# Moving the spare product bank and the first scores of the next unit inside the Mish stretches of a fused attention kernel

## The chip, the cores and the metric

The kernel runs on one core of one Trainium2 chip. A core has five engines, each with its own instruction stream, which wait for each other through semaphores: TensorE (PE in the profile; its weight loads are PEld) multiplies, VectorE (DVE), ScalarE (ACT) and GpSimd (POOL) compute elementwise, SyncE (SP) issues transfers. TensorE writes to PSUM, eight banks of 128 x 512 floats, which VectorE and ScalarE read. The metric is the device time of one execution in microseconds; before the change the median of three runs is 489.91 us (489.81 to 490.08).

## What is computed

Attention over 8 batches of 12 heads, 448 positions and 64 features, with one more term in the softmax's denominator, and on its output a feed-forward layer with the Mish function between its two products:

```python
scores = scale * np.matmul(q, k.transpose(0, 1, 3, 2))
m = np.max(scores, axis=-1, keepdims=True)
e = np.exp(scores - m)
attn = e / (np.sum(e, axis=-1, keepdims=True) + np.exp(-m) + 1e-09)
x = np.matmul(attn, v)                # then 3584 tokens x 768
...
h = x @ w_in                          # 768 x 2048
sp = np.where(h > 20.0, h, np.log1p(np.exp(np.minimum(h, 20.0))))
out = (h * np.tanh(sp)) @ w_out       # 2048 x 768
```

Inputs and output are float32; the matrix products run in bfloat16.

## The kernel before

**Tiling.** Heads are taken in pairs, 48 in all, and three pairs make a unit (sixteen units, two for each batch). The 896 query rows of a pair are seven tiles of 128; their scores are made in four steps, of two, two, two and one tile. A step writes one of three score tiles `sc_tiles` (two PSUM banks each), in turn, so a unit's twelve steps use each tile four times, and the next unit begins with `sc_tiles[0]` again. The last two PSUM banks are `mo_tiles`, handed out by `mo_take` (L107) from a queue, the longest free first; both products of the feed-forward layer and the transposes of the first pairs use them.

**The attention stage of a unit** (L551 to L585). For each of twelve steps ScalarE takes the exponentials of a finished score step (`exps`, L275), then TensorE works off the step's share of the second product (`mm2_part`, L417) for earlier batches, and then `scores_ahead` (L222) issues the scores of coming steps as score tiles come free, each followed by a row maximum on VectorE (L270). At the fourth step of each pair TensorE multiplies an earlier pair's transposed weights by its values into the second bank of that step's score tile (`av_pair`, L344). VectorE's copies out of PSUM are not issued with the product but kept in the list `late`, and issued at the next `flush_late`.

**The Mish stretch between two attention stages** (L591 to L611) goes through eight blocks, `f` = 0 to 7. Each block is one call of `mm1_mish` (L375): a flush of `late`, six matmuls of the first product into one bank (L382), and one Mish activation on ScalarE from there (L388). The bank is taken from `mo_tiles` and given back at once to the queue's end, except in one block, the spare one, which uses the first bank of `sc_tiles[0]`. The first of the two `mo_tiles` in turn is free when the stretch begins; the other still holds the last part of the second product, whose copy (L433) is issued by block 0's flush.

Around the blocks the stretch also does, in program order, which is the order on every engine's queue:

- behind block 0: the denominators of the unit just finished (L296, L300, VectorE) and the normalisation of its first pair (L317, seven VectorE instructions), then the DMA that transposes that pair (L321, issued by SP);
- behind blocks 1, 3 and 5: the eight transposes of a pair of the next unit (`transpose_pair`, L179) into banks of `sc_tiles[2]` and `sc_tiles[1]`, and their copies (`evac_qk`): `qd` by VectorE (L210, two instructions, with the scale), `kT` by ScalarE (L218);
- behind block 3, ahead of that block's transposes: the first score step of the next unit, into `sc_tiles[0]`, with its row maximum;
- further behind block 3: the normalisation of the second pair on VectorE and its transposing DMA;
- behind block 4: the normalisation of the third pair on POOL (L315), ahead of which VectorE copies a small tile for it (L308), and its DMA;
- behind blocks 6 and 7: the second and third score step of the next unit, into `sc_tiles[1]` and `sc_tiles[2]`.

The program has sixteen Mish stretches. The first thirteen do all of this; in the fourteenth there is no next unit any more, and the last two have product blocks alone.

Of the kernel before, what the change touches and what calls it, by code (L numbers as in the profile page):

```python
# [19 lines left out]
def kernel(  # L20
# [24 lines left out]
    FF_U = FF_T // UNITS_PER_B  # L45
    NH = d_model // 2
    SCALE = 1.0 / float(D) ** 0.5
    N_PAIRS = B * HP
    STEPS = 4
# [53 lines left out]
    def flush_late():  # L103
        while late:
            late.popleft()()

    def mo_take():  # L107

        if not mo_free:
            flush_late()  # L110
        return mo_free.popleft()
# [33 lines left out]
    def load_w(n):  # L145
        for _ in range(min(n, len(pieces))):
            dst, src = pieces.popleft()
            nc.gpsimd.dma_start(out=dst, in_=src.rearrange("(a p) c -> p a c", p=128))
# [38 lines left out]
    def evac_qk(p, act=False):  # L187
        if p >= N_PAIRS:
            return
        (q_ps, k_ps), own = qkT[p]  # L190
        mo_free.extend(own)
        qd = q_diag[p % 3]
        kT = qk_pool.tile([128, S], BF16, tag="kT", name="kT")
        if p < DIAG_FROM:
            qT = qd.rearrange("d i h r -> d (i h r)")[:, 0:S]
            qkT[p] = (qT, kT)
            if act:
                nc.scalar.mul(qT, q_ps[:, 0:S], SCALE)
            else:
                nc.vector.tensor_scalar(  # L200
                    out=qT, in0=q_ps[:, 0:S], scalar1=SCALE, scalar2=None, op0=ALU.mult
                )
        else:
            qkT[p] = (qd, kT)
            if p < DIAG_FROM + 3:
                nc.vector.memset(qd[0:64, :, 1, :], 0.0)
                nc.vector.memset(qd[64:128, :, 0, :], 0.0)
            for h in range(2):
                rows = slice(64 * h, 64 * h + 64)
                nc.vector.tensor_scalar(  # L210
                    out=qd[rows, :, h, :],
                    in0=q_ps[rows, 0:S].rearrange("d (i r) -> d i r", i=QB),
                    scalar1=SCALE, scalar2=None, op0=ALU.mult,
                )
        if p == 0 or own and not act:
            nc.vector.tensor_copy(out=kT, in_=k_ps[:, 0:S])
        else:
            nc.scalar.copy(kT, k_ps[:, 0:S])  # L218
# [3 lines left out]
    def scores_ahead(limit):  # L222

        while rg["next"] < limit and rg["used"] < len(sc_tiles):
            rg["used"] += 1
            scores(rg["next"])
            rg["next"] += 1
# [147 lines left out]
    def mm1_mish(b, ff):  # L375
        if ff == 0:
            gT[b] = gT_pool.tile([128, FF_T, S], BF16, tag="gT", name="gT")
        flush_late()
        spare = ff % FF_U == 2
        h_ps = sc_tiles[0][:, 0, :] if spare else mo_take()  # L380
        for dm in range(DM_T):
            nc.tensor.matmul(  # L382
                h_ps[:, 0:S],
                lhsT=w_in_sb[:, dm, ff * 128 : (ff + 1) * 128],
                rhs=xT[b][:, dm, :],
                start=(dm == 0), stop=(dm == DM_T - 1),
            )
        nc.scalar.activation(out=gT[b][:, ff, :], in_=h_ps[:, 0:S], func=AF.Mish)  # L388
        if not spare:
            mo_free.append(h_ps)  # L390
# [26 lines left out]
    def mm2_part(g, i, q0, nq):  # L417

        b0, b1 = 2 * g, 2 * g + 1
        cols, n_cols = slice(q0 * NQ, (q0 + nq) * NQ), nq * NQ  # L420
        st = {}
        if i < 3:
            src, c0 = gT[b0], i * 128
        elif i == 3:
            src, c0 = mids[g], 0
        else:
            src, c0 = gT[b1], i * 128 - S

        def evac():
            if (g, i) not in o_sbs:  # L430
                o_sbs[g, i] = [o_pool.tile([128, d_model], FP32, tag="o_sb", name="o_sb"), 0]
            o_sb, have = o_sbs[g, i]
            nc.vector.tensor_copy(out=o_sb[:, cols], in_=st["o"][:, 0:n_cols])  # L433
            mo_free.append(st["o"])
            o_sbs[g, i][1] = have + nq
            if (g, i) == (B // 2 - 1, 6):
                store_rows(g, i, o_sb, cols)
            elif have + nq == 4:
                store_rows(g, i, o_sb, slice(0, d_model))

        def chunk(f0, f1):
            if f0 == 0:
                flush_late()
                st["o"] = mo_take()
            for ff in range(f0, f1):
                nc.tensor.matmul(  # L446
                    st["o"][:, 0:n_cols],
                    lhsT=src[:, ff, c0 : c0 + 128],
                    rhs=w_out_sb[:, ff, cols],
                    start=(ff == 0), stop=(ff == FF_T - 1),  # L450
                )
            if f1 == FF_T:
                late.append(evac)

        step = 2
        return [(lambda f0=f0: chunk(f0, f0 + step), nq) for f0 in range(0, FF_T, step)]
# [83 lines left out]
    for u in range(UNITS_PER_B, N_UNITS + 2 * UNITS_PER_B):  # L540
        attn = u < N_UNITS
        filler = deque()
        for part in plan.get(u, []):
            filler.extend(mm2_part(*part))
        total, done, acc = sum(w for _, w in filler), 0, 0.0
        p0 = u * UNIT_PAIRS
        if attn and u >= first_mm2:
            av_with.update({p0 + i: p0 + i - UNIT_PAIRS for i in range(UNIT_PAIRS)})
        end = min((u + 1) * UNIT_PAIRS, N_PAIRS) * STEPS

        for n in range(steps):  # L551
            pi, s = divmod(n, STEPS)
            p, idx = p0 + pi, p0 * STEPS + n
            late_tp = u == UNITS_PER_B and n == STEPS
            if late_tp:
                transpose_pair(p0 + 2)
            exps(idx)
            if late_tp:
                evac_qk(p0 + 2)
            if u == UNITS_PER_B + 1:  # L560
                for part in TURN_AT[1].get(n, []):
                    turn_on_pe(*part)
            flush_late()
            acc += weight[n]
            want = int(total * acc / sum(weight) + 1e-6)
            while done < want:
                fn, w = filler.popleft()
                fn()
                done += w
            scores_ahead(end)  # L570
            if n in LOAD_AT:
                load_pair(p0 + LOAD_AT.index(n) + LEAD)
                cast_pair(p0 + LOAD_AT.index(n) + LEAD - 1)
            if u - UNITS_PER_B < len(AV_AT):
                early = AV_AT[u - UNITS_PER_B]
                if n in early:
                    av_pair(early[n])
                if u == UNITS_PER_B:
                    for part in TURN_AT[0].get(n, []):
                        turn_on_pe(*part)  # L580
            elif s == (2 if pi else 0) and N_PAIRS <= p < N_PAIRS + UNIT_PAIRS:
                av_pair(p - UNIT_PAIRS)
            if u - UNITS_PER_B < len(W_AT):
                load_w(W_AT[u - UNITS_PER_B].get(n, 0))
        assert done == total  # L585

        moe = u < N_UNITS + UNITS_PER_B
        b, w = (u - UNITS_PER_B) // UNITS_PER_B, u % UNITS_PER_B
        nxt = p0 + UNIT_PAIRS
        todo = sorted(range(p0, nxt), key=lambda p: p in BY_PE)  # L590
        for f in range(FF_U):  # L591
            if moe:
                mm1_mish(b, w * FF_U + f)
            if u == UNITS_PER_B and f in (2, 6):
                load_w(1)
            if not attn:
                continue
            if f == 0:
                denominators(att[p0]["whole"])
                normalise(todo[0], dma=todo[0] not in BY_PE)  # L600
            if f == 3:
                scores_ahead(min(nxt * STEPS + 1, N_PAIRS * STEPS))
            if f in (1, 3, 5):
                transpose_pair(nxt + f // 2, bank=f // 2 % 2)
                evac_qk(nxt + f // 2)
            if f >= FF_U - 2:
                scores_ahead(min(nxt * STEPS + f - FF_U + 4, N_PAIRS * STEPS))
            if f == 3:
                normalise(todo[1], dma=todo[1] not in BY_PE)
            if f == 4:  # L610
                normalise(todo[2], dma=todo[2] not in BY_PE, on_pool=True)  # L611
        if moe and w == UNITS_PER_B - 1:
            gather_mid(b)
# [32 lines left out]
```

## Time and profile before

| | before |
|---|---|
| median of three runs | 489.91 us |
| the profiled execution, in all | 492.75 us |
| its span, first to last instruction | 491.0 us |
| mean granted TensorE clock | 0.997 |
| TensorE busy | 450.5 us, 92% |
| VectorE busy | 351.3 us, 72% |
| ScalarE busy | 350.2 us, 71% |
| GpSimd busy | 161.5 us, 33% |

All times in the profile are microseconds from the span's start unless they are marked ns. A row of a timeline gives start and length, the engine, the line of the kernel, the operation, what is written and read, the shape, how many instructions were merged (x6), and in brackets the idle time ahead of it with what ended it. A matmul is drawn until its modelled end, which lies behind the start of the next; for the time that TensorE needs, the starts are compared.

### The profile page before, as it was taken

To read this page: it belongs to the slowest core of one execution; us is meant where nothing else is said; L and a number is where in the kernel's file an instruction comes from. 1 tells how busy PE (TensorE), PEld (TensorE's weight loads), DVE (VectorE), ACT (ScalarE), POOL (GpSimd) and SP (SyncE) were. 2 spreads that over 40 slices of the span, in tenths; PEclk is the share of its full clock that TensorE was granted. 3 is DMA by queue.
4 is the path that set the end of the run, shared out by engine and by line. 5 is a ranking of instruction groups with operands and counts; after the bars stand their busy time and mean duration, and the time that the engine had idled before them with its cause. 6 is when DMAs were issued, how large, how long until landed. Compare 5 with 4: busy or idle time off the path is not lost.

```text
span 491.0 us, 8804 instructions
## 1 busy us (share of the span) xinstructions
PE 450.5 (92%) x2992; PEld 248.5 (51%) x2992; DVE 351.3 (72%) x702; ACT 350.2 (71%) x906; POOL 161.5 (33%) x266
## 2 busy tenths in 40 slices
PE   3556898798989999999999999999999999999996
PEld 1222444454644555555655555555556565556563
DVE  4798987978868787878788786878797878420021
ACT  4889678878777887979796878888797979502300
POOL 3622257454412534253413323253425230300000
PEclk9999998999999999999999999999999999999999
DMA  8999999999999999999998979998999686780112
GB/s 212 183 205 228 236 207 221 228 177 236 175 225 263 195 220 188 241 186 267 148 248 187 223 164 210 211 213 227 176 265 179 167 176 140 132 159 21 45 37 93
DMA packets 209452, 92.19 MB, mean 188 GB/s; under 512 B 166272, under 2 KB 205952, under 8 KB 209408
## 3 DMA queue, kind: packets, MB, share of 16 engines
q1 hardware_dynamic: 201920, 85.35, 81.2%
q0 software_dynamic: 7488, 6.29, 8.8%
q8 instruction: 23, 0.38, 0.3%
q14 instruction: 21, 0.17, 0.1%
HBM read 45.61 MB, written 11.01 MB: 115 GB/s over the span
## 4 chain that ended last, share of the span: by engine, by line
PE 68%; DVE 14%; ACT 9%; DMA 4%; issue 2%; SPq 1%; POOL 0%; DVEq 0%; ACTq 0%
PE mo L446 24%; PE mo L382 23%; PE sc L249 8%; ACT en L283 8%; DVE negm L270 7%; PE sc L358 6%; DVE en L317 4%; PE sc L382 3%; PE sc L179 3%; DMA eT<-en 3%; DMA k_f<-in_k_dram 1%; PE mo L358 1%; PE sc L255 1%; DVE xT L367 1%; DVE eT L336 1%
## 5 line engine op out<-in xcount | busy, mean ns | idle before, releaser
L283 ACT ACTIVATE en<-sc,negm 128x448 bf16<-128x448 f32 x336 | 209.7, 637 | 28.7 <-DVE negm L270 16.3
L270 DVE TENSOR_REDUCE negm<-sc 128x2 f32<-128x896 f32 x192 | 182.4, 969 | 61.5 <-PE sc L249 48.7
L446 PE MATMUL mo<-w_out_sb,gT 128*128 128x384 bf16 (+1 forms) x896 | 142.1, 303 | 0.0
L382 PE MATMUL mo<-xT,w_in_sb 128*128 128x448 bf16 x672 | 140.2, 352 | 0.9 <-DVE xT L367 0.9
L388 ACT ACTIVATE gT<-mo 128x448 bf16<-128x448 f32 x112 | 59.4, 543 | 73.5 <-PE mo L382 73.3
L446 PEld LDWEIGHTS <-gT 128*128 128x128 bf16 x896 | 84.0, 98 | 46.8 <-issue 1.3
L382 PEld LDWEIGHTS <-w_in_sb 128*128 128x128 bf16 x768 | 72.8, 98 | 64.9 <-issue 4.2
L315 POOL TENSOR_SCALAR en<-en,rden 128x448 bf16<-128x448 bf16 x98 | 61.7, 649 | 115.8 <-DVE rden L308 106.0
L249 PE MATMUL sc<-kT,qd 128*128 128x448 bf16 x252 | 71.6, 354 | 1.8 <-DVE qd L210 1.5
L162 POOL CAST q_bf<-q_f 112x512 bf16<-112x512 f32 x47 | 29.1, 619 | 121.8 <-DMA q_f<-in_q_dram 105.4
L283 ACT ACTIVATION_READ_ACCUMULATOR en<-sc,negm 128x1 f32 x336 | 69.2, 206 | 0.0
L317 DVE TENSOR_SCALAR en<-en,rden 128x448 bf16<-128x448 bf16 x238 | 67.2, 354 | 0.9
L433 DVE COPY o_sb<-mo 128x384 f32<-128x384 f32 (+1 forms) x64 | 32.1, 502 | 41.3 <-PE mo L446 41.2
L249 PEld LDWEIGHTS <-qd 128*128 128x128 bf16 x252 | 24.0, 97 | 32.1 <-issue 13.9
L358 PE MATMUL sc<-eT,v_bf 112*64 112x448 bf16 x288 | 34.1, 357 | 4.1 <-ACT en L283 2.0
L164 POOL CAST v_bf<-v_f 112x512 bf16<-112x512 f32 x48 | 29.6, 618 | 20.6 <-DMA v_f<-in_v_dram 19.1
L358 PEld LDWEIGHTS <-v_bf 112*64 112x64 bf16 x384 | 21.1, 114 | 25.7 <-issue 16.9
L255 PE MATMUL sc<-kT,qd 64*128 64x448 bf16 x36 | 17.5, 508 | 17.4 <-ACT en L283 16.0
L163 POOL CAST k_bf<-k_f 112x512 bf16<-112x512 f32 x47 | 29.2, 622 | 6.7 <-DMA k_f<-in_k_dram 5.9
L210 DVE TENSOR_SCALAR qd<-sc 64x448 bf16<-64x448 bf16 x72 | 27.8, 386 | 0.9
L218 ACT COPY kT<-sc 128x448 bf16<-128x448 bf16 x39 | 20.8, 534 | 6.8 <-PE sc L179 6.8
L446 PE MATMUL mo<-w_out_sb,mid 128*128 128x384 bf16 x128 | 24.9, 326 | 0.0
(50 smaller groups left out, 306.9 us busy)
## 6 DMA issues: line engine op xcount, KB each, us to landing
q_f<-in_q_dram SPq DMA_DIRECT2D x48, 224.0 KB, 5.5
k_f<-in_k_dram SPq DMA_DIRECT2D x48, 224.0 KB, 5.6
v_f<-in_v_dram SPq DMA_DIRECT2D x48, 224.0 KB, 5.9
w_in_sb<-in_moe_w_in_dram POOLq DMA_DIRECT2D x12, 256.0 KB, 5.6
w_out_sb<-in_moe_w_out_dram POOLq DMA_DIRECT2D x8, 384.0 KB, 8.6
out_dram<-o_sb SPq DMA_DIRECT2D x7, 336.0 KB, 3.5
out_dram<-o_sb SPq DMA_DIRECT2D x8, 288.0 KB, 4.8
out_dram<-o_sb SPq DMA_DIRECT2D x8, 240.0 KB, 3.4
```

The source lines that it names most:

```text
L163: cast_k(out=k_bf, in_=k_f.rearrange(by_t, t=NT))
L164: nc.gpsimd.tensor_copy(out=v_bf, in_=v_f)
L249: nc.tensor.matmul(sc[:, bk, 0:S], lhsT=qT[:, i].rearrange("d h r -> d (h r)"), rhs=kT, start=True, stop=True,)
L270: nc.vector.tensor_reduce(out=negm, in_=sc[:, 0 : len(cols), 0:S], axis=AX.X, op=ALU.max, negate=True)
L283: nc.scalar.activation(out=st["en"][:, :, c, 0:SP_], in_=sc[:, bk, 0:S].rearrange("q (j c) -> q j c", j=NT), func=AF.Exp, bias=st["negm"][ ...
L315: nc.gpsimd.tensor_scalar(scalar2=1.0, op0=ALU.mult, op1=ALU.mult, **args)
L317: nc.vector.tensor_scalar(scalar2=None, op0=ALU.mult, **args)
L358: nc.tensor.matmul(av[h * 64 : (h + 1) * 64, 0:S], lhsT=v_bf[:, h, j * D : (j + 1) * D], rhs=e_h, start=(j == 0), stop=(j == NT - 1),)
L382: nc.tensor.matmul(h_ps[:, 0:S], lhsT=w_in_sb[:, dm, ff * 128 : (ff + 1) * 128], rhs=xT[b][:, dm, :], start=(dm == 0), stop=(dm == DM_T - 1),)
L388: nc.scalar.activation(out=gT[b][:, ff, :], in_=h_ps[:, 0:S], func=AF.Mish)
L433: nc.vector.tensor_copy(out=o_sb[:, cols], in_=st["o"][:, 0:n_cols])
L446: nc.tensor.matmul(st["o"][:, 0:n_cols], lhsT=src[:, ff, c0 : c0 + 128], rhs=w_out_sb[:, ff, cols], start=(ff == 0), stop=(ff == FF_T - 1),)
```

## The change

The spare block, whose product goes to the first bank of `sc_tiles[0]`, is block 1 and not block 2, so block 2 takes the second of the `mo_tiles` where block 1 took it. From block 3 on the banks are as before. The next unit's first score step is issued behind block 4 and not behind block 3; on TensorE it moves past the transposes of the next unit's second pair and block 4's matmuls. On VectorE its row maximum moves past that pair's two scalings and the second pair's normalisation. Nothing else moves.

```diff
@@ -376,7 +376,7 @@
         if ff == 0:
             gT[b] = gT_pool.tile([128, FF_T, S], BF16, tag="gT", name="gT")
         flush_late()
-        spare = ff % FF_U == 2
+        spare = ff % FF_U == 1
         h_ps = sc_tiles[0][:, 0, :] if spare else mo_take()
         for dm in range(DM_T):
             nc.tensor.matmul(
@@ -598,11 +598,11 @@
             if f == 0:
                 denominators(att[p0]["whole"])
                 normalise(todo[0], dma=todo[0] not in BY_PE)
-            if f == 3:
-                scores_ahead(min(nxt * STEPS + 1, N_PAIRS * STEPS))
             if f in (1, 3, 5):
                 transpose_pair(nxt + f // 2, bank=f // 2 % 2)
                 evac_qk(nxt + f // 2)
+            if f == 4:
+                scores_ahead(min(nxt * STEPS + 1, N_PAIRS * STEPS))
             if f >= FF_U - 2:
                 scores_ahead(min(nxt * STEPS + f - FF_U + 4, N_PAIRS * STEPS))
             if f == 3:
```

## The prediction, made before the changed kernel was run

> **What bounds the kernel now.** I read the page first: the span, and the chain of work that ended last.
>
> ```profile
> span 491.0 us, 8804 instructions
> PE 68%; DVE 14%; ACT 9%; DMA 4%; issue 2%; SPq 1%; POOL 0%; DVEq 0%; ACTq 0%
> ```
>
> Two thirds of the end are set by TensorE, so the question is where TensorE still stands still inside the Mish stretches. The program has sixteen of them. I took their bounds from the TensorE timeline (first product matmul of the stretch to first matmul after it) and asked for TensorE's busy time in each; the rows give from:to, length, busy time, the matmuls touched, granted clock, DMA share, GB/s. These are the first fourteen.
>
> ```profile
> 65.89:77.99 12.10, 11.54 (x81) 1.00 1.02 180
> 93.84:105.63 11.79, 11.70 (x78) 1.00 1.18 182
> 120.54:132.31 11.77, 11.58 (x81) 1.00 1.31 193
> 149.20:161.94 12.74, 11.74 (x80) 1.00 1.08 259
> 176.88:188.44 11.56, 11.56 (x79) 1.00 0.84 169
> 203.39:215.14 11.75, 11.74 (x80) 1.00 0.85 199
> 230.25:241.66 11.41, 11.41 (x81) 1.00 0.79 180
> 256.61:268.62 12.01, 11.73 (x79) 1.00 0.87 190
> 283.92:295.48 11.56, 11.56 (x80) 1.00 0.72 151
> 310.43:321.99 11.56, 11.56 (x80) 1.00 0.95 199
> 337.09:348.62 11.53, 11.53 (x80) 1.00 0.84 185
> 363.57:375.13 11.56, 11.56 (x80) 1.00 0.90 182
> 390.07:401.64 11.57, 11.57 (x81) 1.00 0.66 134
> 416.59:425.87 9.28, 9.28 (x50) 1.00 0.48 90
> ```
>
> Thirteen stretches do the same work, eight product blocks, three transposed pairs and three scores, at a granted clock of 1.00, yet they last from 11.41 to 12.74 us. The busy column hides this, because a matmul is drawn longer than its turn; lengths and starts are what to read. The shortest, at 230.25, shows TensorE's timeline with no stall.
>
> ```profile
> 230.25 2.43 PE L382 MATMUL mo<-xT,w_in_sb 128*128 128x448 bf16 x12
> ...
> 232.91 1.30 PE L382 MATMUL sc<-xT,w_in_sb 128*128 128x448 bf16 x6
> ...
> 235.19 0.54 PE L249 MATMUL sc<-kT,qd 128*128 128x448 bf16 x2
> 235.56 0.36 PE L179 MATMUL sc<-ident,q_bf 112*128 112x112 bf16 x4
> ```
>
> From start to start: blocks 2 and 3 take 2.28 us (232.91 to 235.19), so one takes 1.14; blocks 0 and 1 with the first transposed pair take 2.66 (230.25 to 232.91), so the pair takes 0.38; a score step takes 0.37 (235.19 to 235.56). Eight blocks, three pairs and three scores make 9.12 + 1.14 + 1.11 = 11.4: that stretch is saturated. Now the one at 256.61, 0.60 longer: TensorE and its weight loads, then VectorE, then ScalarE.
>
> ```profile
> 256.61 2.59 PE L382 MATMUL mo<-xT,w_in_sb 128*128 128x448 bf16 x12
> 257.90 0.85 PEld L382 LDWEIGHTS <-w_in_sb 128*128 128x128 bf16 x5 [0.25 <-issue]
> 259.43 1.30 PE L382 MATMUL sc<-xT,w_in_sb 128*128 128x448 bf16 x6
> 260.56 1.30 PE L382 MATMUL mo<-xT,w_in_sb 128*128 128x448 bf16 x6
> 262.14 0.55 PE L249 MATMUL sc<-kT,qd 128*128 128x448 bf16 x2 [0.28 <-DVE qd L210]
> ...
> 268.24 0.54 PE L249 MATMUL sc<-kT,qd 128*128 128x448 bf16 x2
> ```
>
> ```profile
> 257.30 0.55 DVE L433 COPY o_sb<-mo 128x384 f32<-128x384 f32 x1
> 259.25 2.12 DVE L317 TENSOR_SCALAR en<-en,rden 128x448 bf16<-128x448 bf16 x7
> 261.30 0.78 DVE L210 TENSOR_SCALAR qd<-sc 64x448 bf16<-64x448 bf16 x2
> 262.73 1.09 DVE L270 TENSOR_REDUCE negm<-sc 128x2 f32<-128x896 f32 x1 [0.65 <-PE sc L249]
> ...
> 264.55 1.81 DVE L317 TENSOR_SCALAR en<-en,rden 128x448 bf16<-128x448 bf16 x7
> ```
>
> ```profile
> 256.09 0.20 ACT L283 ACTIVATION_READ_ACCUMULATOR en<-sc,negm 128x1 f32 x1
> 257.48 0.63 ACT L283 ACTIVATE en<-sc,negm 128x448 bf16<-128x448 f32 x1
> 259.62 0.98 ACT L388 ACTIVATE gT<-mo 128x448 bf16<-128x448 f32 x2
> 260.90 0.57 ACT L388 ACTIVATE gT<-sc 128x448 bf16<-128x448 f32 x1
> ```
>
> There are two stalls. **Stall A**, at block 1: its product tile is the one that the last output part still occupies, and VectorE's copy out of it ends at 257.85. The second half of its weights resumes at 257.90. Block 2 starts 2.82 behind block 0 (256.61 to 259.43), and 2.66 in the stretch without a stall, so the wait is 0.16. **Stall B**, at the first score, behind block 3: that block is through at 260.56 + 1.14 = 261.70, but the score needs qd, whose two scalings stand on VectorE behind seven normalisations and end at 262.08. The score starts at 262.14: 0.44 lost. A and B make the 0.60.
>
> **The change part by part.** No instruction is added or removed; none of what moves issues a DMA.
>
> *Block 1 takes the score tile's bank.* It needs the exponentials of the unit's tenth step, whose accumulator read ends at 256.29. Block 1 is due at 256.61 + 1.14 = 257.75, so the margin is 1.46 us and A is gone. Block 2 takes the late product tile at 259.28 (with the transposes ahead of it), 1.4 us after that copy. I count A in the stretches at 149.20, 176.88, 203.39, 256.61, 283.92, 310.43, 363.57, 390.07 and 416.59; in those at 230.25 and 337.09 the last part is a narrow one whose copy ends earlier, and A is absent.
>
> *Block 3 then comes 0.16 earlier, at 260.41,* and needs the Mish of block 0. That pair of Mish instructions starts at 259.62 and the second ends at 260.60; one of them alone takes about 0.54, so the first ends near 260.17. Margin 0.24, of which a semaphore takes 0.05 (262.08 to 262.14 above). I take zero; the other bound is that all of A comes back here, 0.16 in each of nine stretches. Block 4's tile now waits for block 2's Mish, which stands behind block 1's and a copy of kT and ends by 261.47; block 4 is due at 261.94. Nothing is lost.
>
> *The first score moves behind block 4,* to 261.94 + 1.14 = 263.08, a full 1.0 us after qd at 262.08. The cover is one transposed pair and one block, 1.52 us. The longest B is that at 149.20, where the seven normalisations are slow beside POOL's casts:
>
> ```profile
> 151.78 2.92 DVE L317 TENSOR_SCALAR en<-en,rden 128x448 bf16<-128x448 bf16 x7
> 152.27 0.62 POOL L162 CAST q_bf<-q_f 112x512 bf16<-112x512 f32 x1 [0.88 <-DMA q_f<-in_q_dram]
> ```
>
> There the normalisations end at 154.70 and the two scalings (0.78) near 155.48; the score will be due 6.47 behind the stretch's start (256.61 to 263.08), at 155.67. It fits.
>
> *Behind the moved score on VectorE.* The score's row maximum now stands behind the second pair's scaling and normalisation instead of ahead of them; then come the small copy for POOL and the third qd. At 256.61: second scaling to 262.9, normalisation (1.81) to 264.7, maximum (1.09) to 265.8, 0.2 allowed for the copy to 266.0, third qd (0.78) to 266.8. The last score needs that qd and is due at 267.64: margin 0.85. The middle pair's transposing DMA can start up to 1.6 us earlier (its normalisation ends at 264.7, not 266.36); POOL's normalisation moves with the stretch. No order on SP's or POOL's queue changes. The first exponentials of the next unit stand behind the last Mish and a table load, 2 us after all of this.
>
> A rule that speaks against this: by the Trainium skill, page "SBUF — State Buffer", section "Who interferes with whom", a VectorE tensor_scalar in a two-port mode and a GpSimd instruction lock each other out for a whole instruction. The 2.92 row above, against 1.81 without casts beside it, agrees in kind. With three casts of 0.62 each in full on the moved normalisation, an estimate from that rule, the third qd would be 1.86 late and the last score 1.0.
>
> **The sum.** Stretches 149.20 to 390.07 are ten; their lengths sum to 117.25, ten times 11.41 is 114.10, so 3.15 goes, and 0.16 at 416.59: **3.3 us**. Does it stay gone? The attention stage between two stretches lasts 176.88 - 161.94 = 14.94, 203.39 - 188.44 = 14.95, 256.61 - 241.66 = 14.95, 310.43 - 295.48 = 14.95: the same behind a stretch of 12.74 as behind one of 11.41. It hangs on the stretch's end alone, so what a stretch saves is saved. For the first three stretches (0.69, 0.38 and 0.36 over 11.41) it is less clear, since one transfer is late behind them:
>
> ```profile
>   DMA eT<-en: 1.9, 1
> ...
> DMA to landing us min/median/max: 6.0/6.4/12.4
> ```
>
> This is the only wait of TensorE for a transposed pair, and the stage behind 132.31 is the one that it stretches (149.20 - 132.31 = 16.89, 1.94 over 14.95); I take the longest landing, 12.4 us where 6.4 is the median, for this transfer's. The 0.36 of the stretch at 120.54 comes after that transfer's issue and is swallowed. The other two, 0.69 + 0.38 = 1.07 at most, move that issue earlier. If the landing follows, 1.1 is kept; if the DMA engines (share 1.31 there) land it at the same time, none. I take 0.6, nearer to the first, since the loads that crowd it move with the program. Together 3.9 us of 491.0. The profiled execution took 492.75 in all, the median of the three runs is 489.91; the stalls are the same program's, so I take the 3.9 off the median: **486.0 us**.
>
> **The rivals.**
>
> *Block 3 takes A back and the early part is lost.* If Mish of block 0 ends after 260.36 there, block 3 waits. For it: the margin of 0.24 is the smallest here. Against: with A gone, the stretch at 230.25 already runs block 3 at this distance and shows no wait. Only B of the ten stretches is left, 3.15 - 8 x 0.16 = 1.9: 488.0 us.
>
> *The saving reappears elsewhere.* The DMA queues are busy throughout (shares of 0.66 to 1.31 above), so transfers might hold the units at their present pace. Against: one DMA wait of TensorE in the whole run. Then 489.9.
>
> *Slower: the tile that is called free isn't.* If block 1's bank were released only by the unit's last exponential (257.48 + 0.63 = 258.11, read out about 0.1 later), block 1 would start near 258.25, not 257.75: 0.5 in each of the eleven stretches from 149.20 on, 5.5 us, against 3.9 gained: 491.5. It decides from 0.36 a stretch (3.9 / 11). Against: the bank's own last reader ends at 256.29, the twelfth step being in another tile.
>
> *Casts meet the moved normalisation.* At the measured 2.92 instead of 1.81 the third qd is 1.11 late, 0.26 beyond its margin; in some six stretches that have casts at their head, 1.5 given back: 487.5. Against: three casts from 152.27 on end near 154.1, and the second normalisation there begins some 2 us later. By the rule of the Trainium skill's page "SBUF — State Buffer", with 1.0 in each of six, it would be 492.0, an estimate.
>
> **How the numbers follow.** The forecast gets 0.77, the loss at block 3 0.08, the reappearance 0.06, the busy bank 0.05, the casts 0.04. Low end: all stalls of the first three stretches kept, 3.3 + 1.43 = 4.7, 485.2, and 0.2 for spread: 485.0. High end: the first rival's 488.0 and 0.2: 488.2. What is left out is the two last outcomes at 489.9 and beyond, 0.11. A change of 0.2%, 1 us, is about what a measurement of this kernel can tell from none. Faster by more than that: 0.77 + 0.08 + 0.04 = 0.89, less a little for a case I don't see, 0.88; within it 0.06; slower 0.06.
>
> **What would show it.** Right: every stretch up to 390.07 about 11.4 us long; the twelve matmuls before the first transposes split in a mo and a sc group, no pause of weights at block 1; no wait of the first score for qd; attention stages still 14.95. Wrong: a pause ahead of block 1 or block 3, the last score waiting for qd, attention stages longer than 14.95, or the transposed pair behind the third stretch landing at the same time as before.

## The result and the profile after

The changed kernel takes 487.79 us (median of 17 runs, 485.11 to 490.55) against 489.91 us for the kernel before, measured beside it (17 runs, 488.45 to 492.12). The ratio is 0.9953, 95% interval 0.9936 to 0.9970: 1.5 to 3.1 us less. The time lies in the forecast's range and on its side; the 3.9 us of the forecast were too many. The spread of single runs is wide, in part because the start varies: in fourteen profiles of this study the first Mish stretch begins between 62.7 and 65.9 us, though up to there the order of work is the same in all of them. Of the 6.4 us between the spans 491.0 and 484.6, 2.6 are such a difference at the start (65.89 against 63.28) and have nothing to do with the change.

The page after:

```profile
span 484.6 us, 8804 instructions
PE 72%; DVE 12%; ACT 7%; DMA 5%; issue 2%; SPq 1%; POOL 0%; DVEq 0%; POOLq 0%
```

TensorE's share of the chain is 72% here and was 68% before, but nothing follows from that: second profiles of the two kernels have 66% and 69%, the other way round. The lengths of the stretches decide. The same view of the first fourteen Mish stretches as before (from:to, length, TensorE's busy time, clock, DMA share, GB/s):

```profile
63.28:75.06 11.78, 11.63 (x81) 1.00 1.04 177
90.93:102.41 11.48, 11.48 (x79) 1.00 1.37 198
117.54:128.94 11.40, 11.40 (x80) 1.00 1.31 188
144.93:157.29 12.36, 11.56 (x79) 1.00 1.09 273
172.23:183.64 11.41, 11.41 (x81) 1.00 0.94 171
198.59:209.99 11.40, 11.40 (x79) 1.00 0.83 187
225.10:236.50 11.40, 11.40 (x80) 1.00 0.91 190
251.45:262.97 11.52, 11.52 (x80) 1.00 0.90 196
278.26:289.67 11.41, 11.41 (x81) 1.00 0.80 166
304.62:316.02 11.40, 11.40 (x79) 1.00 0.94 190
331.13:342.54 11.41, 11.41 (x82) 1.00 0.90 199
357.49:368.89 11.40, 11.40 (x79) 1.00 1.00 184
383.83:395.24 11.41, 11.41 (x80) 1.00 0.75 146
410.19:419.47 9.28, 9.24 (x50) 1.00 0.48 90
```

Most stretches are at the forecast's 11.4 us. Three rows are not as forecast: the fourth is still 12.36, the eighth 11.52, and the fourteenth has not moved from 9.28. The fourth, on TensorE and then on VectorE:

```profile
147.59 2.44 PE L382 MATMUL mo<-xT,w_in_sb 128*128 128x448 bf16 x12
150.83 0.36 PE L179 MATMUL sc<-ident,q_bf 112*128 112x112 bf16 x4 [0.80 <-DVE qd L210]
151.22 1.30 PE L382 MATMUL mo<-xT,w_in_sb 128*128 128x448 bf16 x6
152.35 0.54 PE L249 MATMUL sc<-kT,qd 128*128 128x448 bf16 x2
```

```profile
147.21 2.87 DVE L317 TENSOR_SCALAR en<-en,rden 128x448 bf16<-128x448 bf16 x7
149.99 0.78 DVE L210 TENSOR_SCALAR qd<-sc 64x448 bf16<-64x448 bf16 x2
```

Blocks 2 and 3 run through without a wait, and the first score, moved behind block 4, doesn't wait either. What waits are the transposes of the next unit's second pair, which now stand directly behind block 3, where the score stood: they start at 150.83, just after the first pair's scalings end at 150.77. They don't read what those scalings write, and they write the other bank of the tile that the scalings read. In the order of TensorE's instructions the wait for VectorE has moved from the score to them. The list gives the first instructions of each group (`Ldweights` a weight load, `Matmult` a matmul) with the engine whose semaphore they wait for, first of the kernel before, then of the changed one; the transposes' weight loads, which wait for POOL's casts in both, are left out:

```
L249 Ldweights qd0                     waits for VectorE
L249 Matmult   sc0 <- kT, qd0          waits for ScalarE
L179 Matmult   sc2 <- ident, q_bf      no wait

L179 Matmult   sc2 <- ident, q_bf      waits for VectorE
...
L249 Matmult   sc0 <- kT, qd0          no wait
```

In the fourteenth stretch the rows show why block 3 is late. TensorE's three rows begin block 0, block 1 and block 2; ScalarE's row is the Mish of block 0.

```profile
410.19 1.30 PE L382 MATMUL mo<-xT,w_in_sb 128*128 128x448 bf16 x6
411.33 1.30 PE L382 MATMUL sc<-xT,w_in_sb 128*128 128x448 bf16 x6
412.46 2.82 PE L382 MATMUL mo<-xT,w_in_sb 128*128 128x448 bf16 x13
```

```profile
413.21 0.54 ACT L388 ACTIVATE gT<-mo 128x448 bf16<-128x448 f32 x1
```

Block 1 has no pause any more, but there are no transposes behind it in this stretch, so block 3 is due at 412.46 + 1.14 = 413.60, ahead of the end of block 0's Mish at 413.75. It takes back what block 1 saved.

The transposed pair that was late behind the third stretch is still late, by less: TensorE waits 1.0 us for it (1.9 before), and the longest landing is 11.6 us (12.4 before).

```profile
  DMA eT<-en: 1.0, 1
...
DMA to landing us min/median/max: 6.1/6.5/11.6
```

### The profile page after: what moved, and what is told of

Its sections match the earlier page's. It is cut to its first block, busy times and chain, and to the rows that moved or that the text cites. A ratio compares the mean times of both kernels' runs of the same rounds, so it can differ in the third digit from the quotient of the medians.

```text
span 484.6 us, 8804 instructions
## 1 busy us (share of the span) xinstructions
PE 448.3 (93%) x2992; PEld 249.0 (51%) x2992; DVE 347.1 (72%) x702; ACT 348.8 (72%) x906; POOL 160.6 (33%) x266
## 4 chain that ended last, share of the span: by engine, by line
PE 72%; DVE 12%; ACT 7%; DMA 5%; issue 2%; SPq 1%; POOL 0%; DVEq 0%; POOLq 0%
PE mo L446 25%; PE mo L382 24%; PE sc L249 8%; DVE negm L270 7%; ACT en L283 6%; PE sc L358 6%; PE sc L382 3%; PE sc L179 3%; DMA eT<-en 2%; DVE en L317 2%; DMA k_f<-in_k_dram 1%; PE mo L358 1%; DMA q_f<-in_q_dram 1%; PE sc L255 1%; DVE eT L336 1%
## 5 line engine op out<-in xcount | busy, mean ns | idle before, releaser
L283 ACT ACTIVATE en<-sc,negm 128x448 bf16<-128x448 f32 x336 | 209.3, 636 | 26.9 <-DVE negm L270 15.2
L388 ACT ACTIVATE gT<-mo 128x448 bf16<-128x448 f32 x112 | 61.2, 547 | 77.4 <-PE mo L382 77.1
L249 PE MATMUL sc<-kT,qd 128*128 128x448 bf16 x252 | 71.5, 354 | 0.3 <-ACT en L283 0.2
L317 DVE TENSOR_SCALAR en<-en,rden 128x448 bf16<-128x448 bf16 x238 | 64.2, 343 | 0.9
L249 PEld LDWEIGHTS <-qd 128*128 128x128 bf16 x252 | 24.5, 97 | 28.9 <-issue 13.5
L358 PEld LDWEIGHTS <-v_bf 112*64 112x64 bf16 x384 | 20.9, 114 | 24.9 <-issue 16.9
L179 PEld LDWEIGHTS <-q_bf 112*128 112x128 bf16 x192 | 14.5, 104 | 17.8 <-DVE q_bf L162 4.4
```

Source lines behind the costliest of these rows:

```text
L179: nc.tensor.transpose(by_s[s][:, t * SP_ : (t + 1) * SP_], src[:, t].rearrange("p h d -> p (h d)"), ident[:SP_, :SP_],)
L249: nc.tensor.matmul(sc[:, bk, 0:S], lhsT=qT[:, i].rearrange("d h r -> d (h r)"), rhs=kT, start=True, stop=True,)
L283: nc.scalar.activation(out=st["en"][:, :, c, 0:SP_], in_=sc[:, bk, 0:S].rearrange("q (j c) -> q j c", j=NT), func=AF.Exp, bias=st["negm"][ ...
L317: nc.vector.tensor_scalar(scalar2=None, op0=ALU.mult, **args)
L358: nc.tensor.matmul(av[h * 64 : (h + 1) * 64, 0:S], lhsT=v_bf[:, h, j * D : (j + 1) * D], rhs=e_h, start=(j == 0), stop=(j == NT - 1),)
```

## The experiments

Two theories. **Theory 1** is the prediction: stalls A and B are both removed. **Theory 2** is read from the rows above: A is removed, B is passed on to the transposes. Four kernels went together first. Ratios are against the kernel before, run beside them.

**The kernel before, again** (no edit).

> The kernel before once more, for a second profile of it and for the spread. Both theories: 489.9 us within 1.5, stall A of 0.16 us in the nine stretches that had it, stall B in about the same stretches but of other sizes, since it hangs on POOL's casts. The time up to the first Mish stretch (65.89 us in the profile before, 63.28 after) differs from run to run by 2 to 3 us, with no change to the kernel.

Measured: 489.53 us, ratio 0.9993 (0.9967 to 1.0020). The start is at 63.25 us instead of 65.89. Of the ten steady stretches, the fourth to the thirteenth, B occurs in the fourth, seventh, eighth and tenth (0.82, 0.22, 0.14 and 0.21 us), not in the same as before (1.17 in the fourth, 0.17 in the sixth, 0.44 in the eighth, 0.11 in the eleventh). B is a stall of changing place and size, and one profile's list of it can't be carried over stretch by stretch. POOL's casts beside the normalisations are only one of its causes: in the eighth and tenth stretch here the seven normalisations take the usual 1.81 us, but begin 2.67 and 2.74 us after the stretch's start instead of 2.28, and in the sixth and eleventh of the profile before it is the same (1.81 us, begun at 2.70 and 2.48).

**The change, again** (no edit).

> The changed kernel once more. Theory 1 (the prediction): A and B are both gone, 486.0 us, and the pause of 0.97 us in the stretch at 144.93 was a chance of one run. Theory 2: the second pair's transposes, which now stand in TensorE's order where the score stood, wait for the same qd scalings; A is gone, B is not. Then every stretch with slow normalisations shows a pause ahead of those transposes, block 3 waits about 0.2 us in the fourteenth stretch, and the time is 487.5 to 488.5 us.

Measured: 487.22 us, ratio 0.9968 (0.9945 to 0.9990). The pause ahead of the second pair's transposes is there again, in the fourth, fifth, seventh and eighth stretch: 0.26, 0.30, 0.17 and 0.52 us, 1.3 in sum. It was no chance of one run. The fourteenth stretch lasts 9.29. This is the pattern of theory 2; the time is 0.3 us below the range that it gave.

**Only the spare block.**

```diff
-        spare = ff % FF_U == 2
+        spare = ff % FF_U == 1
```

> The spare block is block 1, the first score stays behind block 3. Theory 1: only A goes, 1.4 us less at most, B stays, so 488.5 us, and the change is 1.9 us or more faster than this. Theory 2: this is all that the change does, so it is as fast as the change within 0.5 us; where B exists A's 0.16 is swallowed by it.

**Only the first score.**

```diff
-            if f == 3:
-                scores_ahead(min(nxt * STEPS + 1, N_PAIRS * STEPS))
             if f in (1, 3, 5):
                 transpose_pair(nxt + f // 2, bank=f // 2 % 2)
                 evac_qk(nxt + f // 2)
+            if f == 4:
+                scores_ahead(min(nxt * STEPS + 1, N_PAIRS * STEPS))
```

> The spare block stays block 2, the first score moves behind block 4. Theory 1: B goes, A stays, 487.4 to 488.0 us, the steady stretches 11.57 us long at most. Theory 2: nothing goes, 489.9 us within 0.5; stretches with slow normalisations still last longer than 11.57 us, with the pause ahead of the second pair's transposes.

Both were run a second time:

> The moved spare block alone, once more: block 1 without a pause, pauses behind block 3 of 2.5 to 3.3 us in all thirteen stretches, third stretch and stage together 28 to 29.4 us, 489 us within 0.7.

> The moved score alone, once more, since one profile is little for a wait whose size changes from run to run. If moving the score takes B away, no pause behind block 3; by theory 2 pauses of 1 to 1.8 us in all thirteen stretches; third stretch and stage together 26.4 to 27.4 us; 488.2 us within 0.7.

Measured: the spare block alone 489.05 and 489.94 us, ratios 0.9998 (0.9973 to 1.0023) and 1.0006 (0.9989 to 1.0022); the score alone 488.20 and 488.55 us, 0.9982 (0.9960 to 1.0004) and 0.9980 (0.9961 to 1.0000). So theory 2's claim that the spare block is all of the change is wrong too: by time the spare block can't be told from nothing. The score's move lowers both medians by some 0.9 us, but its two intervals still reach 1, so it alone isn't clear of noise either; its 488.2 us lies between what the two theories gave. The list of TensorE's waits shows who waits for the scalings of qd, in sum, times and longest, in the first run of the spare block alone:

```profile
PE sc L249 <- DVE qd L210: 2.4, 2, 1.3
```

and in the second run of the score alone:

```profile
PE sc L179 <- DVE qd L210: 0.7, 1, 0.7
```

It is the score (L249) in the first and the transposes (L179) in the second, each in the place behind block 3. In the second run of the score alone, the fourth stretch:

```profile
150.16 0.36 PE L179 MATMUL sc<-ident,q_bf 112*128 112x112 bf16 x4 [0.71 <-DVE qd L210]
```

The pauses are smaller on the whole where the score is moved, but not gone, as the table below shows: the score alone has stretches of 12.04 and 12.43 us, where theory 1 gave 11.57 at most.

**Both transposes of the second pair in one tile.** If the wait is owed to writing the tile that the scalings read, it goes when that pair's q and k are both transposed into the second bank of `sc_tiles[1]`, half a bank each. First with the change:

```diff
-        ps = mo_take() if bank is None else sc_tiles[2][:, bank, :]
+        ps = mo_take() if bank is None else sc_tiles[1 if bank else 2][:, bank, :]
```

> The changed kernel, with both transposes of the second pair in the second bank of sc_tiles[1] (one half for q, one for k), so that they no longer write the tile from which the first pair's qd is scaled. Theory 2 (the pause ahead of them is a wait for that scaling): the pause is gone, the stretches 149.20 to 390.07 of the numbering before are 11.4 us each, and the sum over these ten falls from 115.2 us (mean of two profiles of the change) to 114.1. Theory 1 (no such wait): no difference from the change.

Measured: 484.31 us, ratio 0.9895 (0.9875 to 0.9915), 4 to 6 us less than before. The fourth to seventh stretch and the fourteenth:

```profile
143.37:154.77 11.40, 11.40 (x79) 1.00 1.08 291
169.72:181.12 11.40, 11.40 (x79) 1.00 1.00 183
196.07:207.48 11.41, 11.41 (x80) 1.00 0.90 188
222.59:234.00 11.41, 11.41 (x81) 1.00 0.92 206
...
407.22:416.50 9.28, 9.24 (x50) 1.00 0.48 91
```

All thirteen stretches are without a pause behind block 3, with normalisations of up to 2.57 us among them, and the ten steady ones sum to 114.1 us: the forecast's figure, reached with an edit that the change doesn't contain. The waits follow the tile: in the profile of the change the second pair's q transposes carry a wait for VectorE and its k transposes one for ScalarE in every one of the thirteen stretches; with one tile the first of them carries one for ScalarE, which copies the first pair's kT out of the other bank of that tile, and none for VectorE. Then in the kernel before, without the change:

> The kernel before, with both transposes of the second pair in the second bank of sc_tiles[1] and nothing else. There the first score stands behind block 3 and reads qd itself. Theory 2: no gain, pauses behind block 3 of 2 to 3 us in all thirteen stretches, 489.5 us within 0.7. If one tile pays by itself, 3 us less.

Measured: 489.82 us, ratio 0.9995 (0.9977 to 1.0014). Its pauses sum to 1.5 us over the thirteen stretches, under the 2 to 3 expected, but the score waits as before, since there it truly needs qd:

```profile
PE sc L249 <- DVE qd L210: 0.7, 1, 0.7
```

So neither the score's place nor the transposes' tile removes B alone; it takes both. (The run without any pause also has the spare block moved, which by itself leaves the pauses at 1.9 and 1.6 us.) In this kernel another wait shows. The second pair's kT now lies in one bank with its q, and ScalarE's copy of it waits for VectorE's scalings of that q; here in the second stretch, on ScalarE and then on TensorE:

```profile
99.15 0.53 ACT L218 COPY kT<-sc 128x448 bf16<-128x448 bf16 x1 [2.51 <-DVE qd L210]
```

```profile
99.73 0.36 PE L179 MATMUL sc<-ident,k_bf 112*128 112x112 bf16 x4 [0.32 <-ACT kT L218]
```

The third pair's k transposes, into the first bank of `sc_tiles[1]`, start only when ScalarE has read the second pair's kT from the second bank of that tile. It is again a wait for a reader of the other bank, this time on another engine. In the steady stretches it costs some 0.06 us each (11.62 us where the kernel before has 11.56), which is why the ten of this run stay at 117.0 us in the table below.

**The last three stretches.** With the change and one tile, products also went to other score tiles where no next unit follows:

```diff
-        h_ps = sc_tiles[0][:, 0, :] if spare else mo_take()
+        last = b * FF_T + ff >= (N_UNITS - 1 - UNITS_PER_B) * FF_U
+        spare = spare or last
+        h_ps = sc_tiles[ff % 3 if last else 0][:, 0, :] if spare else mo_take()
```

> As the kernel before it in this group, and in the last three stretches, which have no next unit, every product goes to the first banks of the three score tiles in turn. If block 3 of the fourteenth stretch waits for block 0's Mish because no transposes stand between, that stretch falls from 9.28 to 9.08 us and the two after it stay at 9.08; if something else holds it, it stays at 9.28.

Measured: 486.16 us, ratio 0.9938 (0.9919 to 0.9958). The fourteenth stretch is 9.08 us, but the stage ahead of it grew from 14.95 to 16.59. In the fourteenth stretch `ff % 3` begins with 2, so block 0 stood on the tile of the unit's last score step, and had to wait for its exponentials:

```profile
PE sc L384 <- ACT en L283: 1.5, 1, 1.5
```

This is the mechanism of the prediction's slower rival: a spare bank that isn't free yet costs 1.5 us at one place. With blocks 1, 2 and 3 on the three score tiles in turn, and block 0 on a product tile again:

```diff
-        spare = ff % FF_U == 1
-        h_ps = sc_tiles[0][:, 0, :] if spare else mo_take()
+        f = ff % FF_U
+        last = b * FF_T + ff >= (N_UNITS - 1 - UNITS_PER_B) * FF_U
+        spare = f in (1, 2, 3) if last else f == 1
+        h_ps = sc_tiles[f - 1][:, 0, :] if spare else mo_take()
```

> The change, both transposes of the second pair in the second bank of sc_tiles[1], and in the last three stretches blocks 1, 2 and 3 in the first banks of the three score tiles, block 0 in a product tile again. If the 1.64 us that the stage ahead of the fourteenth stretch gained in the run with the tail came from block 0 waiting for the unit's last exponential, that stage is 14.95 us again, the fourteenth stretch is 9.08, and the time is 0.2 us under that of the change with one tile (484.3): 484.1 us.

Measured: 485.48 us where 484.1 was expected, ratio 0.9910 (0.9881 to 0.9939); the stage is 14.95 again and the fourteenth stretch has no pause:

```profile
410.35:419.43 9.08, 9.08 (x50) 1.00 0.47 88
```

By time it can't be told from the version without the tail (the intervals overlap, and 0.2 us is below what these runs show). Both beat the kernel before. Against the change (0.9936 to 0.9970) the version without the tail is clearly faster; the interval of this one just touches the change's.

**What the score's move brings in the first third.** Two more edits of the kernel before. The last four weight pieces earlier:

```diff
-{3: 1, 5: 1, 7: 1, 9: 1})
+{2: 4})
```

> The kernel before, with the last four pieces of the second weights issued together at the third step of the attention stage, not at the fourth, sixth, eighth and tenth. If the long stage behind the third stretch (16.9 and 16.6 us before, 16.0 and 15.0 with the change) is long because these pieces land late and hold up the transposing DMA, third stretch and stage together fall from 28.3 us to about 26.5 without the change; if the change's gain there comes from the score's place alone, they stay at 28 to 28.7.

and TensorE's order left alone, with only the row maximum of the first score moved:

```diff
+        if rg.get("hold"):
+            held.append(row_max)
+        else:
+            row_max()
...
+            if f == 4:
+                while held:
+                    held.popleft()()
```

> The kernel before, with TensorE's order untouched: the first score stays behind block 3 and the spare block is block 2, only the score's row maximum on VectorE moves behind block 4. If the moved score pays through VectorE's queue (the second pair's scaling and normalisation no longer stand behind a maximum that waits for TensorE), this gives what moving the score alone gave: outside the time up to the first stretch 2.6 us less, with the second stretch at 11.5 and third stretch and stage together at 26.4 to 27.4 us. If it pays through TensorE's order, 0 to 0.5 us.

Measured: early weights 488.28 us, ratio 0.9981 (0.9967 to 0.9995); third stretch and stage together 26.9 us, as expected, but the stage ahead of them grew by 0.95 us, with a wait of TensorE of 1.5 us for a transposed pair, so part is given back. The maximum alone: 489.59 us, ratio 1.0004 (0.9980 to 1.0028); the second stretch fell to 11.51, as expected, but third stretch and stage stayed at 28.7. VectorE's order alone doesn't bring it.

The profiles side by side, in us, from the starts on TensorE's timeline. "Start" is the time up to the first stretch, "first" the three first stretches with the stages behind them, "ten" the fourth to thirteenth stretch, "pauses" those behind block 3 in these ten, "third" the third stretch with its stage.

| kernel | start | rest | first | ten | pauses | third |
|---|---|---|---|---|---|---|
| before | 65.9 | 425.1 | 83.3 | 117.2 | 1.9 | 28.7 |
| before, again | 63.3 | 424.5 | 83.3 | 116.7 | 1.4 | 28.0 |
| spare block alone | 63.1 | 423.7 | 83.2 | 116.0 | 1.9 | 29.4 |
| the same, again | 65.0 | 423.5 | 83.3 | 115.7 | 1.6 | 28.1 |
| score alone | 63.8 | 422.2 | 81.9 | 115.8 | 0.5 | 26.4 |
| the same, again | 63.2 | 421.9 | 81.0 | 116.4 | 1.1 | 26.4 |
| the change | 63.3 | 421.3 | 81.6 | 115.1 | 1.1 | 27.4 |
| the change, again | 64.4 | 420.7 | 80.9 | 115.3 | 1.3 | 26.4 |
| maximum alone | 64.4 | 425.2 | 83.2 | 117.5 | 2.1 | 28.7 |
| early weights | 62.7 | 423.2 | 82.5 | 116.1 | 0.8 | 26.9 |
| before, one tile | 63.3 | 422.6 | 81.4 | 117.0 | 1.0 | 26.4 |
| change, one tile | 63.2 | 418.4 | 80.1 | 114.1 | 0.0 | 26.4 |
| change, one tile, first tail | 63.5 | 420.3 | 81.1 | 114.1 | 0.0 | 27.3 |
| change, one tile, second tail | 65.2 | 419.4 | 81.3 | 114.1 | 0.0 | 26.4 |

A profile is one run of 6 to 17, and not always a middle one: the single run of the kernel before with one tile is 2 us quicker than its median. The rows are good for where time goes; for how much, the ratios decide.

## Why the prediction was right in its side and wrong in its sizes

**Stall A, right, mis-sized at the end.** Block 1 on the score tile's bank has no pause in any of the changed profiles, and the ten stretches lose about 1.1 us by it (117.0 in the mean of the kernel before to 115.9 with the spare block alone). The step that put 0.16 us down for the fourteenth stretch failed: its margin of 0.24 at block 3 was worked out with a transposed pair between blocks 1 and 2, and this stretch has none. There the first rival came true, at one place of nine.

**Stall B, the step that failed.** The prediction put the score "a full 1.0 us after qd" and gave it a cover of "one transposed pair and one block". That was right of the score, which waits nowhere. It didn't ask what comes to stand in the freed place behind block 3. These are the transposes of the second pair; in the kernel before the score stood ahead of them and took their wait upon itself, so they showed none. With the change the pauses in the ten stretches are 1.1 and 1.3 us, of 1.9 and 1.4 before, where zero was forecast; one tile makes them zero. That TensorE waits for the scalings there is shown by the wait's end (150.77 to 150.83), by the instruction order and by its disappearance. That it is a wait for the tile as a whole, and not for the bank, is supported by two things: it passes from VectorE to ScalarE when the transposes change tiles, and the kernel before with one tile shows such a wait for ScalarE. The traces don't hold the counts that are waited for, so it isn't proved. Why the pauses are somewhat smaller with the score moved is open; the single sums overlap (1.0 to 2.1 with the score unmoved and the weights in their place, 0.5 to 1.3 with it moved).

**The first three stretches, too small.** The sum took 0.6 us, bounded by 1.1; the profiles show 2.0 (83.3 to 81.6 and 80.9). The bound held only the stretches' own excess. The late transposed pair itself came earlier: the wait behind the third stretch fell from 1.9 us to 1.0 in one profile and to none in the other. The prediction had "swallowed" for what lies behind that transfer and didn't see that an earlier second pair moves what feeds it. What goes with it: POOL's normalisation in the second stretch ends 12.35 to 12.71 us ahead of the third stretch's start in the eight profiles (of those with the weights in their place) whose stage lasts 14.95 to 15.98 us, among them all with the score moved, and 12.0 us ahead in the four with 16.2 to 16.9 (both of the kernel before, both of the spare block alone). But the kernel before with one tile is among the eight, at 14.95 us, with the score unmoved: moving the score isn't the only way to the short stage. POOL's end releases the third transposing DMA, the loads behind it on SP's queue, the casts and the last weight pieces on POOL's; with these pieces issued early the stage behind the third stretch lasts 14.95 us without the change. The maximum alone breaks the row: POOL ends 12.3 us ahead, and the stage is 17.2. So that the last weights hold up the transfer is supported by one experiment, and how the score's move clears them is open.

**The sum came out near for the wrong reasons.** In the profiles, outside the start, the change saves 3.8 us (425.1 and 424.5 to 421.3 and 420.7), as forecast: 1.8 in the ten stretches where 3.15 were, none at the fourteenth where 0.16 was, and 2.0 in the first three where 0.6 was. By the medians it is about 2. Both profiled runs of the change lie under its median by 0.3 and 1.5 us, so part of the gap is the choice of runs; the rest wasn't settled. The median, 487.79 us, lies nearest to the first rival's 488.0, and that too is chance: its mechanism occurred at one place of nine.

**The rivals.** Block 3 taking A back: once, in the fourteenth stretch. The saving reappearing elsewhere: no, the ten stages behind the fourth to thirteenth stretch sum to 150.1 or 150.2 us in both profiles of the kernel before and both of the change. (Not all of them last 14.95 us, as the four that the prediction read do: three have 15.1 to 15.3 in all four profiles.) The busy bank: not in the change, as its margin of 1.46 us said. The casts: no, in the stretch with the slow first normalisation they end at 149.70, the moved second one starts at 152.05 and takes 1.81 us, and no last score waits for qd. So the rule of the Trainium skill's page "SBUF — State Buffer", section "Who interferes with whom", had nothing to act on there.

## What to carry to other kernels

Moving an instruction out of a wait doesn't remove the wait until the next instruction in that queue has been looked at: one that shows no wait behind a stalled neighbour may have been covered by it. List for each engine what stands behind the moved instruction, and which tile, not only which bank, it writes.

A margin worked out in a typical pass of a loop has to be worked out again for the last passes, where the work between two steps is missing. And where single runs spread over 5 us, compare profiles by stretch and leave the start out, before a difference of spans is read as an effect.

## What was not expected of the hardware

The time up to the first Mish stretch varied from 62.7 to 65.9 us over kernels that are the same up to there, and the third stretch's stage from 14.95 to 17.20: both go with waits for transfers. Up to the first stretch TensorE waits 2.3 us for POOL's casts of q, which wait for their loads, where the stretch begins at 65.9, and 0.4 us where it begins at 62.7; behind the third stretch it waits 2.2 us for a transposed pair where the stage lasts 17.20, and not at all where it lasts 14.95. The DMA engines are full meanwhile (shares of 1.02 to 1.37 in the first three stretches of the two profiles listed above). Beside three casts of POOL, seven normalisations of VectorE took 2.87 us in the change and 2.92 in the kernel before, instead of 1.81. From the end of VectorE's scalings to the start of the waiting transposes 0.06 us passed (150.77 to 150.83).
